# An attention and expert kernel: the attention steps of batches 2 to 7 in another order and spacing, and one finishing step split over two items

## The chip, the cores and the metric

The kernel runs on one core of a Trainium2 chip. The core has TensorE (PE, matrix products), VectorE (DVE), ScalarE (ACT), GpSimd (POOL) and SyncE (SP, which issues most of the transfers). The metric is device time of the whole kernel in microseconds, as the median of several runs; less is better.

## The reference

Two stages. An attention without a score matrix (softmax of q over its 64 features, softmax of k over its 576 positions) gives x, and a gated feed-forward layer follows:

```python
q_s = softmax(q, over head_dim);  k_s = softmax(k, over seq)      # q, k, v: 8 x 8 x 576 x 64
kv  = einsum('bhsd,bhse->bhde', k_s, v)
x   = einsum('bhsd,bhde->bhse', q_s, kv)  ->  4608 x 512
h   = x @ w_in                                                    # 512 x 2048
sp  = max(h, 0) + log1p(exp(-abs(h)))
out = (h * erf(sp)) @ w_out                                       # 2048 x 512
```

## The kernel before

**The layer's work is cut into 48 items.** The 4608 rows of x come as 12 blocks of 384 (three to a pair of batches), and each block takes four items, one for each group of 512 hidden features. Item n multiplies block n//4 by its group of w_in (`mm1`, called with k = 0 to 3), takes softplus and erf (`softplus`, `erf`, through `act`), multiplies and halves into two f16 parts (`gmul`, `ghi`, `glo`), and multiplies by w_out (`mm2`, called for three row tiles). Values are held as two f16 halves, so each product takes three passes. `mm1` needs only seven products of half size instead of eight; they go to three accumulation banks: `pY_n`, `pX_n` and `pZ_n`, of which `pX` is used for four of the seven. Each product must be read out before its bank's next one may start: VectorE reads at L1015 (Y), L1017 and L1025 (X, first and third), L1028 (Z, second), ScalarE at L1020 (Z, first), L1022 and L1030 (X, second and fourth). The line numbers are those of the kernel before.

**x is made by the attention of each batch**, a generator `attention(b)` that is run one step at a time between the products of the items. For one batch it takes k's maximum over the positions (`k_max`, elementwise on VectorE into `asc`), transposes it on TensorE (`kT_b`, L528), reduces it on VectorE (`km_b`, L532), spreads it again over the rows on TensorE (`kB_b`, L543), subtracts it from k's two halves and its tail (`k_b_0` and `k_b_1` at L709, `kt` at L714), subtracts q's maximum from q's two halves (`q_b_0` and `q_b_1`: maximum at L464, subtraction at L465; odd batches also have `qt`, the tail), takes the exponentials (L348 through `act`), multiplies k by v (`kv_b_0`, `kv_b_1`, L564), normalizes q and turns it (`turn` or `rw`, L629 and L630), and makes x (L685, copied into the block `x_i` at L453).

**What sets the order.** Each step ends with a `yield` of its share, a number from `SHARES`, and `pace` runs steps until the sum of the shares reaches a goal that grows evenly with the items. The Tile scheduler then puts the instructions of each engine in a row, so that neighbours in the code may change places. All exponentials and the softplus and erf of items 2 to 36 are held in one chain, in the order in which they are written. Once a block is whole, `finish` (two calls, k = 0 and 1) cuts it into the operands `x7_i` of `mm1`: k = 0 makes parts 0 to 2, k = 1 does four subtractions (L392) and makes parts 3 to 6, each part as a first half on ScalarE (L299) and a second on VectorE (L300). Products Y and the first X read parts 0 and 1, the first Z reads part 3. From item 9 on both calls stand in the item with n % 4 == 2; `x7_2`, for items 8 to 11, is called for in item 7 by the hand-written table `SPLITS`.

Of the kernel before, what the change touches and what calls it, by code (L numbers as in the profile page):

```python
# [13 lines left out]
ALU = mybir.AluOpType  # L14
# [41 lines left out]
def attn_moe_kernel(  # L56
# [21 lines left out]
    NG = NF // FG  # L78
# [3 lines left out]
    NBK = PT // T  # L82
# [260 lines left out]
    def act(out_, in_, func, chain=True, **kw):  # L343

        with ExitStack() as es:
            if chain and last[0] is not None:
                es.enter_context(tc.issue_after(last[0]))
            i = nc.scalar.activation(out_, in_, func, **kw)  # L348
        if chain:
            last[0] = i.ins  # L350
        return i
# [19 lines left out]
    x_next = [1]  # L371
# [77 lines left out]
    def bank(name):  # L449
        return psa.tile([P, 512], F32, tag="bk", name=name)  # L450
# [4 lines left out]
    def hd(t):  # L455
        return t.rearrange("p h d -> p (h d)")

    def rows(t):
        return t.rearrange("p t h d -> p (t h) d")

    def q_sub(t, g, name):

        m = at.tile([P, g], F32, tag=f"qm{g}", bufs=1, name=f"{name}_m")
        nc.vector.tensor_reduce(m, t, axis=AX.X, op=ALU.max)  # L464
        nc.vector.tensor_tensor(  # L465
            t, t, m[:, :, None].to_broadcast([P, g, D]), op=ALU.subtract
        )
# [44 lines left out]
    def k_max(b, ks, kt):  # L512

        kmax = asc[:, 0].rearrange("p (h d) -> p h d", h=H)
        k2 = asc[:, 1].rearrange("p (t h d) -> p t h d", t=2, h=4)
        for hf in range(2):
            nc.vector.tensor_tensor(k2, ks[hf][:, 0:2], ks[hf][:, 2:4], op=ALU.max)
            nc.vector.tensor_tensor(
                kmax[:, hf * 4:hf * 4 + 4, :], k2[:, 0], k2[:, 1], op=ALU.max
            )  # L520
        nc.vector.tensor_tensor(kmax[kt[1]], kmax[kt[1]], kt[0], op=ALU.max)
        return kmax

    def k_max_T(b, kmax):
        bk = bank(f"kT_{b}")
        km2 = hd(kmax)
        for c in range(NC4):
            nc.tensor.transpose(  # L528
                bk[:, c * P:(c + 1) * P], km2[:, c * P:(c + 1) * P], ident
            )  # L530
        km = at.tile([P, NC4], F32, tag="km", bufs=1, name=f"km_{b}")
        nc.vector.tensor_reduce(  # L532
            km, bk.rearrange("p (c s) -> p c s", c=NC4), axis=AX.X, op=ALU.max
        )
        return km
# [14 lines left out]
    def kv_mm(b, hf):  # L550


        d, kt_ = bat[b], bat[b - b % 2]["kt"]
        bk = bank(f"kv_{b}_{hf}")
        for c in range(2):
            for t in range(TM + 1):
                for a in range(2):
                    h = 2 * a + c
                    if t < TM:
                        kk, vv = d["k"][hf][:, t, h, :], d["v"][hf][:, h, t, :]  # L560
                    else:

                        kk, vv = kt_[:, 4 * hf + h, :], vtail[:, 4 * hf + h, :]
                    nc.tensor.matmul(  # L564
                        bk[a * D:(a + 1) * D, c * W:(c + 1) * W], kk, vv,
                        start=(t == 0), stop=(t == TM),
                    )
        return bk
# [7 lines left out]
    def kv_norm(b, hf, bk):  # L576
        if b < E32:
            kvf = kv32[b]
        else:
            kvf = asc[:, 0, :NC4 * D].rearrange("p (c e) -> p c e", c=NC4)  # L580
        bat[b]["kvf"] = kvf
        bkv = bk[:, :2 * W].rearrange("p (c w) -> p c w", c=2)
        rd = at.tile([P, 2, 1], F32, tag="rd", bufs=1, name=f"rd_{b}_{hf}")
        nc.vector.tensor_scalar_add(rd, bkv[:, :, D:], 1e-9)
        nc.vector.reciprocal(rd, rd)
        cs = slice(2 * hf, 2 * hf + 2)
        nc.vector.tensor_tensor(
            kvf[:, cs, :], bkv[:, :, :D], rd.to_broadcast([P, 2, D]), op=ALU.mult
        )
# [107 lines left out]
    def attention(b):  # L697
        d, j, p = bat[b], b % 2, b // 2
        even = bat[b - j]
        tl = slice(j * TAIL, (j + 1) * TAIL)  # L700
        ks, qs, kt = d["k"], d["q"], even["kt"][tl]
        kmax = k_max(b, ks, (kt, tl))
        yield SHARES[0]
        km = k_max_T(b, kmax)
        q_sub(rows(qs[0]), 16, f"q_{b}_0")
        yield SHARES[1]
        kb = k_max_rows(b, km)
        for hf in range(2):
            nc.vector.tensor_tensor(  # L709
                ks[hf], ks[hf],  # L710
                kb[:, None, hf * 4:hf * 4 + 4, :].to_broadcast([P, TM, 4, D]),
                op=ALU.subtract,
            )
        nc.vector.tensor_tensor(kt, kt, kb[tl], op=ALU.subtract)  # L714
        yield SHARES[2]
        q_sub(rows(qs[1]), 16, f"q_{b}_1")
        if j == 1:
            q_sub(even["qt"], H, f"qt_{p}")
        yield SHARES[3]
        for t in (*ks, kt, qs[0], qs[1], *([even["qt"]] if j == 1 else [])):  # L720
            act(t, t, AF.Exp, chain=b > 1)
        yield SHARES[4]
        kv_norm(b, 0, kv_mm(b, 0))
        if b > 1:
            d["v"].append(load_half(v, "v", b, 1))
        q_norm(rows(qs[0]), 16, f"q_{b}_0", b)
        yield SHARES[5]
        if b >= QDMA:
# [74 lines left out]
    def attention_rest():  # L803
        for b in range(1, B):
            yield from attention(b)
# [407 lines left out]
    def pace(at_n):  # L1213


        at_n += LEAD
        k = NBK * NG + NG
# [11 lines left out]
    FIN = 2  # L1229
    for n in range(N32, N + 2):  # L1230
        m0, m1, m2 = n < N, n - 1 < N, n - 2 < N
        if m1:
            tok(f"U{n - 1}")
        for i in range(4):
            if m0:
                tok(f"m{n}.{i}")
            if N32 < n <= N and i < 2:
                tok(f"{'IO'[i]}{n - 1}")
            if m0 and n % NG == FIN and n > 2 * NG and i < 2 and x_next[0] < NP * NBK:
                tok(f"f{fi[0]}")  # L1240
                fi[0] += 1
            if m2 and i < 3:
                tok(f"M{n - 2}.{i}")
                pace(n + (i + 1) / NTT)
        for o in SPLITS.get(n, "").split():
            tok(o)
        if m0:
            tok(f"T{n}")
            tok(f"G{n}")
# [32 lines left out]
```

## Time and profile before

| | us |
|---|---|
| median of 3 runs | 829.68 |
| the runs | 829.53 to 832.42 |
| the profiled execution, its own time | 833.75 |
| span in the profile of that execution | 831.9 |
| TensorE busy | 805.1 (97% of the span) |
| VectorE busy | 626.3 (75%) |
| ScalarE busy | 503.1 (60%) |
| mean granted TensorE clock | 0.997 |

The profile shows one execution. Engines run side by side and wait for each other through semaphores; an idle time is put down to the instruction that ended it. The profiled execution is 4.07 us above the median of the runs. Times within the profile count from the start of the span.

### The profile page before, as it was taken

Reading aid. Unit: us, or ns where it says so; the run is one execution under the profiler, and the core shown is the slowest. Engines: PE = TensorE matmul, PEld = TensorE weight load, DVE = VectorE, ACT = ScalarE, POOL = GpSimd, SP = SyncE. Lnnn points to the kernel's source line nnn. Section 1 sums busy time; section 2 is a strip of 40 time slices with the busy share of each in tenths; the row PEclk is TensorE's granted clock in tenths of the full one; section 3 lists DMA queues with packets and bytes.
Section 4 is the critical chain, followed back from the end, with each engine's and each line's share of the span. In section 5 each row is a group of like instructions: output and inputs, shape, how many; then the busy total and the mean of one; then the engine's idle time right before and its main releaser. Section 6 shows DMA issues by size and latency. Waiting matters only on the chain.

```text
span 831.9 us, 15626 instructions
## 1 busy us (share of the span) xinstructions
PE 805.1 (97%) x6594; PEld 546.3 (66%) x6594; DVE 626.3 (75%) x892; ACT 503.1 (60%) x642; POOL 15.9 (2%) x37
## 2 busy tenths in 40 slices
PE   5999999999899999999999999999999999999996
PEld 4555456666676667667667667766776767767762
DVE  6999799999987869757976679857875656544643
ACT  3697678885676566546744646655764555544432
POOL 2101000000000000000000000000000000000000
PEclk9999999999999999999999999999999999999999
DMA  9996721053136206111371205311230100100101
GB/s 260 408 224 181 189 48 39 2 132 72 45 85 129 74 7 142 50 26 28 91 128 43 65 1 106 92 26 27 64 52 14 39 1 2 39 1 2 39 1 39
DMA packets 145509, 62.61 MB, mean 75 GB/s; under 512 B 134688, under 2 KB 136736, under 8 KB 145440
## 3 DMA queue, kind: packets, MB, share of 16 engines
q1 hardware_dynamic: 143264, 53.23, 26.3%
q0 software_dynamic: 2176, 8.39, 2.9%
q8 instruction: 52, 0.85, 0.4%
q14 instruction: 17, 0.14, 0.0%
HBM read 45.09 MB, written 9.44 MB: 66 GB/s over the span
## 4 chain that ended last, share of the span: by engine, by line
PE 55%; DVE 26%; ACT 8%; issue 4%; DMA 4%; SPq 2%; POOL 0%; ACTq 0%; DVEq 0%; POOLq 0%
PE o L1129 26%; PE pX L1003 13%; PE pZ L1003 7%; DVE G L1083 3%; PE pY L1003 3%; DVE H L1101 3%; ACT G L348 3%; ACT L348 2%; DVE wt L300 2%; SPq L419 2%; DVE x L300 2%; DVE H L1097 2%; PE pX L1042 1%; DVE wt L326 1%; DVE q L478 1%
## 5 line engine op out<-in xcount | busy, mean ns | idle before, releaser
L1129 PE MATMUL o<-wt,H 128*128 128x512 f16 x1548 | 355.8, 379 | 1.8 <-DVE H L1097 1.3
L1003 PEld LDWEIGHTS <-wt 128*128 128x128 f16 x3612 | 301.5, 98 | 38.9 <-issue 16.3
L1129 PEld LDWEIGHTS <-H 128*128 128x128 f16 x1548 | 149.2, 98 | 154.0 <-DVE H L1097 1.8
L1003 PE MATMUL pX<-x,wt 128*128 128x192 f16 x2064 | 199.5, 246 | 5.3 <-DVE H L1025 2.6
L348 ACT ACT_TABLE_LOAD x104 | 133.4, 1283 | 9.3 <-DVE H L1028 7.5
L1083 DVE SCALAR_TENSOR_TENSOR G<-G,small,H 128x1536 f32<-128x1536 f32 x44 | 79.9, 1816 | 53.1 <-ACT G L348 52.8
L1030 ACT COPY H<-pX 128x384 f32<-128x384 f32 x43 | 20.4, 474 | 140.5 <-PE pX L1003 132.4
L1003 PE MATMUL pZ<-x,wt 128*128 128x192 f16 x1032 | 101.2, 248 | 0.0
L348 ACT ACTIVATE G<-H,U 128x768 f32<-128x768 f32 (+1 forms) x58 | 71.0, 1242 | 22.1 <-DVE H L1028 21.5
L1101 DVE TENSOR_TENSOR H<-G,H 128x1536 f16<-128x1536 f32 x43 | 75.5, 1755 | 0.9
L348 ACT ACTIVATE G<-G 128x1536 f32<-128x1536 f32 x48 | 71.2, 1484 | 0.5
L1003 PE MATMUL pY<-x,wt 128*128 128x192 f16 x516 | 49.6, 246 | 0.1
L453 ACT ACTIVATE x<-x 128x384 f32<-128x384 f32 (+1 forms) x52 | 16.2, 397 | 48.4 <-PE x L685 48.4
L1028 DVE TENSOR_TENSOR H<-pZ,H 128x384 f32<-128x384 f32 x43 | 23.7, 551 | 26.2 <-PE pZ L1003 26.2
L1015 DVE COPY H<-pY 128x384 f32<-128x384 f32 x43 | 23.8, 552 | 25.7 <-PE pY L1003 25.7
L1097 DVE CAST H<-G 128x1536 f16<-128x1536 f32 x43 | 41.1, 956 | 0.8
L299 ACT ACTIVATE x<-x 128x768 f16<-128x768 f32 (+1 forms) x44 | 32.9, 764 | 13.6 <-DVE x L392 13.5
L300 DVE SCALAR_TENSOR_TENSOR x<-x,x 128x768 f16<-128x768 f32 (+1 forms) x44 | 37.3, 851 | 3.2 <-ACT x L299 3.2
L1145 DVE TENSOR_SCALAR ob<-o,V 128x512 f32<-128x512 f32 x29 | 21.7, 747 | 19.7 <-PE o L1129 19.7
L1017 DVE TENSOR_TENSOR H<-pX,H 128x384 f32<-128x384 f32 x43 | 23.8, 554 | 12.9 <-PE pX L1003 12.1
L464 DVE TENSOR_REDUCE q_m<-q 128x16 f32<-128x1024 f32 x14 | 17.1, 1219 | 15.7 <-DMA q<-in_q_dram 15.6
L1042 PE MATMUL pX<-x,wt 128*128 128x384 f32 x80 | 28.3, 488 | 0.2 <-DVE wt L219 0.2
(183 smaller groups left out, 784.7 us busy)
## 6 DMA issues: line engine op xcount, KB each, us to landing
out_dram<-ob SPq DMA_DIRECT2D x32, 256.0 KB, 2.3
vbuf<-in_v_dram SPq DMA_DIRECT2D x56, 128.0 KB, 3.2
q<-in_q_dram SPq DMA_DIRECT2D x56, 128.0 KB, 3.2
k<-in_k_dram SPq DMA_DIRECT2D x56, 128.0 KB, 3.5
wt<-in_moe_w_out_dram POOLq DMA_DIRECT2D x5, 1024.0 KB, 7.4
wt<-in_moe_w_in_dram SPq DMA_DIRECT2D x4, 1024.0 KB, 12.3
wt<-in_moe_w_out_dram SPq DMA_DIRECT2D x2, 1024.0 KB, 15.9
H_raw<-in_k_dram SPq DMA_DIRECT2D x2, 512.0 KB, 5.0
```

Source lines behind the costliest of these rows:

```text
L299: nc.scalar.activation(hi, src, AF.Copy, scale=s)
L300: nc.vector.scalar_tensor_tensor(lo, src, s, hi, op0=ALU.mult, op1=ALU.subtract)
L348: i = nc.scalar.activation(out_, in_, func, **kw)
L1003: nc.tensor.matmul(o, w[wl][:, c, a * P:(a + 1) * P], x[:, xl, xi, c, :], start=(new and a == 0 and c == 0 and i == 0), stop=(c == 1 and i ...
L1015: nc.vector.tensor_copy(C[0, 0], bank2("Y"))
L1017: add(C[0, 0], bank2("X"), C[0, 0], op=ALU.add)
L1028: add(C[0, 1], bank2("Z"), C[0, 1], op=ALU.add)
L1042: nc.tensor.matmul(ph[:, :T], w[:, c, a * P:(a + 1) * P], x[:, c, :], start=(c == 0), stop=(c == NC4 - 1),)
L1083: nc.vector.scalar_tensor_tensor(flat(s["G"]), flat(s["G"]), GA32 if n < N32 else GA[:, g:g + 1], flat(s["H"]), op0=ALU.mult, op1=ALU.mult,)
L1097: nc.vector.tensor_copy(flat(s["gh"]), flat(s["G"]))
L1101: nc.vector.tensor_tensor(flat(s["gl"]), flat(s["G"]), flat(s["gh"]), op=ALU.subtract)
L1129: nc.tensor.matmul(o, s[gt][:, a, ts_], w[wl][:, a, :], start=(first_ and a == 0 and i == 0), stop=(last_ and a == FG - 1 and i == 2),)
```

## The change

For batches 2 to 7 `attention` gets five shares of its own, `EVEN`, in place of the first four of `SHARES` (sums 2.76 in both). Before, a step of 2.51 stood behind `k_max`, then kT, km and the first half of q, kB and k's subtractions right behind, and 0.16 later the second half of q. Now kT and km come 0.8 behind `k_max`, kB and k's subtractions 0.8 later, the first half of q 0.5 later, the second half with the tail 0.4 later, and 0.26 later the exponentials. The exponentials and all later steps stand as before. Batches 0 and 1 keep the old order. `finish` is now called with k = 0 in the item with n % 4 == 2 and with k = 1 in the one with n % 4 == 3 (from item 9 on), each behind the second product call (i == 1). No instruction is added or removed.

```diff
+EVEN = [0.8, 0.8, 0.5, 0.4, 0.26]
...
-        yield SHARES[0]
-        km = k_max_T(b, kmax)
-        q_sub(rows(qs[0]), 16, f"q_{b}_0")
-        yield SHARES[1]
-        kb = k_max_rows(b, km)
-        for hf in range(2):
-            nc.vector.tensor_tensor(
...
-        nc.vector.tensor_tensor(kt, kt, kb[tl], op=ALU.subtract)
-        yield SHARES[2]
-        q_sub(rows(qs[1]), 16, f"q_{b}_1")
-        if j == 1:
-            q_sub(even["qt"], H, f"qt_{p}")
-        yield SHARES[3]
...
+        else:
+
+            yield EVEN[0]
+            km = k_max_T(b, kmax)
+            yield EVEN[1]
+            k_sub(k_max_rows(b, km))
+            yield EVEN[2]
+            q_subs(0)
+            yield EVEN[3]
+            q_subs(1)
+            yield EVEN[4]
...
-            if m0 and n % NG == FIN and n > 2 * NG and i < 2 and x_next[0] < NP * NBK:
+            if m0 and n % NG >= FIN and n > 2 * NG and i == 1 and x_next[0] < NP * NBK:
```

The scheduler makes of it the following rows at three places. The numbers at the end of a tile's name tell its buffers apart. In the rows of after, lines up to L700 stand one higher than before, and those of `mm1`, `gmul`, `ghi`, `glo` 18 higher (L1043 is L1025 of before, L1101 is L1083, L1115 is L1097, L1119 is L1101); k's subtractions are L706 and L711.

First, VectorE in items 19 and 20, batch 5. Before:

```order
L1083 SCALAR_TENSOR_TENSOR G_19_3727<-G_19_3727,small_81,H_19_3566 128x1536
L300 SCALAR_TENSOR_TENSOR x7_6_4115<-x_6_3503,x7_6_4115 128x768
L1097 CAST H_19_3566<-G_19_3727 128x1536
L1025 TENSOR_TENSOR H_20_3732<-pX_20_3747,H_20_3732 128x2x192
L1101 TENSOR_TENSOR H_19_3566<-G_19_3727,H_19_3566 128x1536
L300 SCALAR_TENSOR_TENSOR x7_6_4115<-x_6_3503,x7_6_4115 128x768
L532 TENSOR_REDUCE km_5_3844<-kT_5_3839 128x4
L1028 TENSOR_TENSOR H_20_3732<-pZ_20_3774,H_20_3732 128x2x192
```

After:

```order
L1101 SCALAR_TENSOR_TENSOR G_19_3727<-G_19_3727,small_81,H_19_3558 128x1536
L393 TENSOR_TENSOR x_6_3495<-x_6_3495 128x2x192
L1115 CAST H_19_3558<-G_19_3727 128x1536
L706 TENSOR_TENSOR k_5_0_3165<-k_5_0_3165,kB_5_3821 128x1024
L1119 TENSOR_TENSOR H_19_3558<-G_19_3727,H_19_3558 128x1536
L706 TENSOR_TENSOR k_5_1_3170<-k_5_1_3170,kB_5_3821 128x1024
L711 TENSOR_TENSOR kt_2_2214<-kt_2_2214,kB_5_3821 64x512
L1043 TENSOR_TENSOR H_20_3732<-pX_20_3747,H_20_3732 128x2x192
L1046 TENSOR_TENSOR H_20_3732<-pZ_20_3781,H_20_3732 128x2x192
```

The maxima `km_5` and the three subtractions from k (L706, L711) now stand ahead of the third readout of X of item 20 (L1043), and the conversions of `x7_6` (L301) behind it.

Second, ScalarE in item 15, batch 4. Before:

```order
L1020 COPY H_15_2833<-pZ_15_2885 128x2x192
L1022 COPY H_15_2833<-pX_15_2848 128x2x192
L348 ACT_TABLE_LOAD
L348 ACTIVATE k_4_0_2204<-k_4_0_2204 128x1024
L348 ACTIVATE k_4_1_2209<-k_4_1_2209 128x1024
L348 ACTIVATE kt_2_2214<-kt_2_2214 64x512
L348 ACTIVATE q_4_0_2411<-q_4_0_2411 128x1024
L348 ACTIVATE q_4_1_2636<-q_4_1_2636 128x1024
L1030 COPY H_15_2833<-pX_15_2848 128x2x192
```

After:

```order
L349 ACT_TABLE_LOAD
L349 ACTIVATE k_4_0_2204<-k_4_0_2204 128x1024
L349 ACTIVATE k_4_1_2209<-k_4_1_2209 128x1024
L349 ACTIVATE kt_2_2214<-kt_2_2214 64x512
L349 ACTIVATE q_4_0_2411<-q_4_0_2411 128x1024
L349 ACTIVATE q_4_1_2636<-q_4_1_2636 128x1024
L1038 COPY H_15_2843<-pZ_15_2893 128x2x192
L1040 COPY H_15_2843<-pX_15_2858 128x2x192
L630 CAST rw_86<-q_4_0_2411 128x1024
L1048 COPY H_15_2843<-pX_15_2858 128x2x192
```

The five exponentials and their table load moved ahead of the first two readouts of item 15 (L1038 and L1040).

Third, VectorE at the end of batch 2's steps, where block 2 is finished for item 8. Before:

```order
L585 RECIPROCAL rd_2_1_1399<-rd_2_1_1399 128x2
L1028 TENSOR_TENSOR H_7_1217<-pZ_7_1309,H_7_1217 128x2x192
L587 TENSOR_TENSOR asc_85<-kv_2_1_1378,rd_2_1_1399 128x128
L300 SCALAR_TENSOR_TENSOR x7_2_1450<-x_2_787,x7_2_1450 128x768
L630 TENSOR_TENSOR turn_0_1374<-q_2_0_775,turn_0_1374 128x1024
L593 TENSOR_REDUCE mx_2_1420<-asc_85 128x1
L1015 COPY H_8_1470<-pY_8_1471 128x2x192
L471 TENSOR_REDUCE q_2_1_r_1567<-q_2_1_803 128x16
```

After:

```order
L588 TENSOR_TENSOR asc_85<-kv_2_1_1378,rd_2_1_1399 128x128
L393 TENSOR_TENSOR x_2_787<-x_2_787 128x2x192
L594 TENSOR_REDUCE mx_2_1420<-asc_85 128x1
L393 TENSOR_TENSOR x_2_787<-x_2_787 128x2x192
L1033 COPY H_8_1470<-pY_8_1471 128x2x192
L393 TENSOR_TENSOR x_2_787<-x_2_787 128x2x192
L472 TENSOR_REDUCE q_2_1_r_1567<-q_2_1_803 128x16
L393 TENSOR_TENSOR x_2_787<-x_2_787 128x2x192
L301 SCALAR_TENSOR_TENSOR x7_2_1450<-x_2_787,x7_2_1450 128x768
L1035 TENSOR_TENSOR H_8_1470<-pX_8_1485,H_8_1470 128x2x192
L301 SCALAR_TENSOR_TENSOR x7_2_1450<-x_2_787,x7_2_1450 128x768
```

The subtractions on `x_2` (L393), and with them the last two conversions of `x7_2` (L301), stood ahead of these rows before and now stand among L594 (the maximum of kv), the readouts of item 8 and the sum over `q_2_1` (L472).

## Rows read from the trace of the kernel before

**Rows 1.** Page of the profile, part 1: busy us of each engine (share of the span) and its instructions.
```profile
PE 805.1 (97%) x6594; PEld 546.3 (66%) x6594; DVE 626.3 (75%) x892; ACT 503.1 (60%) x642; POOL 15.9 (2%) x37
```

**Rows 2.** The view of who waited for whom, TensorE alone, from 130 to 830 us. Columns: the engine and line that waited, what released it, us in total, times, the longest in us.
```profile
PE pX L1003 <- DVE H L1025: 2.6, 4, 1.2
PE kB L543 <- DVE km L532: 2.0, 1, 2.0
PE pX L1003 <- ACT H L1022: 1.7, 2, 1.4
...
PE kv L564 <- ACT k L348: 0.6, 1, 0.6
```

**Rows 3.** The timeline of TensorE, one row at batch 3's spreading of the maxima (`kB_3`). Columns: start us, us, engine, line, operation, tiles, shape, count, and in brackets the idle time in us just before it with what released it.
```profile
225.50 0.70 PE L543 MATMUL kB<-ident,km 128*128 128x128 f32 x4 [2.04 <-DVE km L532]
```

**Rows 4.** Busy time by stretch, around the two longest gaps of TensorE. Columns: stretch and its us, then busy us and count of PE, PEld, DVE, ACT, POOL, the granted TensorE clock (1.00 is 2.4 GHz), DMA share, GB/s.
```profile
226.00:227.00 1.00, 1.00 (x9) 0.95 (x7) 0.77 (x1) 0.00 (x0) 0.00 (x0) 0.50 0.00 0
227.00:228.00 1.00, 1.00 (x8) 0.95 (x7) 1.00 (x2) 0.51 (x1) 0.00 (x0) 0.50 0.00 0
228.00:230.00 2.00, 2.00 (x18) 1.92 (x17) 1.84 (x3) 1.90 (x3) 0.00 (x0) 0.65 0.00 0
400.00:402.00 2.00, 0.65 (x8) 0.65 (x8) 2.00 (x3) 2.00 (x3) 0.00 (x0) 1.00 0.00 0
```

**Rows 5.** The same view for the 20 us in which batch 2's last steps lie.
```profile
180.00:200.00 20.00, 19.64 (x163) 13.19 (x161) 20.00 (x37) 13.52 (x14) 0.00 (x0) 1.00 0.45 93
```

**Rows 6.** The timeline of VectorE from the last step of `x7_2` (177.70 us) on. Columns as in rows 3; the tile names are without their numbers (`x<-x,x` is `x7_2`).
```profile
177.70 0.95 DVE L300 SCALAR_TENSOR_TENSOR x<-x,x 128x768 f16<-128x768 f32 x1
178.57 1.22 DVE L630 TENSOR_TENSOR turn<-q,turn 128x1024 f16<-128x1024 f32 x1
179.70 0.41 DVE L593 TENSOR_REDUCE mx<-asc 128x1 f32<-128x256 f32 x1
180.03 0.54 DVE L1015 COPY H<-pY 128x384 f32<-128x384 f32 x1
180.50 1.20 DVE L471 TENSOR_REDUCE q_r<-q 128x16 f32<-128x1024 f32 x1
```

**Rows 7.** The timeline of TensorE: the first product of item 8 that reads the second half of `x7_2` (`pZ_8`).
```profile
182.33 1.15 PE L1003 MATMUL pZ<-x,wt 128*128 128x192 f16 x12
```

**Rows 8.** Page, part 5: the group of the half conversions on ScalarE. Columns: line, engine, operation, tiles and shape, count, then busy us and mean ns of one, then the idle time just before them and what ended most of it.
```profile
L299 ACT ACTIVATE x<-x 128x768 f16<-128x768 f32 (+1 forms) x44 | 32.9, 764 | 13.6 <-DVE x L392 13.5
```

**Rows 9.** Groups of instructions by line, VectorE: the subtraction for k's tail. Columns as in rows 8.
```profile
L714 DVE TENSOR_TENSOR kt<-kt,kB 64x512 f32<-64x512 f32 x7 | 4.8, 683 | 0.1
```

**Rows 10.** The timeline of VectorE in items 19 and 20, with batch 5's steps (`q_5_1`, `km_5`, `k_5_0`). Columns as in rows 3.
```profile
379.97 1.22 DVE L464 TENSOR_REDUCE q_m<-q 128x16 f32<-128x1024 f32 x1 [1.80 <-DMA q<-in_q_dram]
...
381.58 1.22 DVE L465 TENSOR_TENSOR q<-q,q_m 128x1024 f32<-128x1024 f32 x1
...
383.18 1.74 DVE L392 TENSOR_TENSOR x<-x 128x384 f32<-128x384 f32 x3
384.84 1.81 DVE L1083 SCALAR_TENSOR_TENSOR G<-G,small,H 128x1536 f32<-128x1536 f32 x1
...
387.44 0.95 DVE L1097 CAST H<-G 128x1536 f16<-128x1536 f32 x1
388.30 0.55 DVE L1025 TENSOR_TENSOR H<-pX,H 128x384 f32<-128x384 f32 x1
388.77 1.75 DVE L1101 TENSOR_TENSOR H<-G,H 128x1536 f16<-128x1536 f32 x1
...
391.31 0.68 DVE L532 TENSOR_REDUCE km<-kT 128x4 f32<-128x512 f32 x1
...
395.66 1.21 DVE L709 TENSOR_TENSOR k<-k,kB 128x1024 f32<-128x1024 f32 x1
```

**Rows 11.** The timeline of TensorE in the same place: the last X product of item 20, a Y product, a part of mm2, `kB_5`, a Z product, and the third X product of item 21 with the 1.39 us ahead of it.
```profile
389.23 1.15 PE L1003 MATMUL pX<-x,wt 128*128 128x192 f16 x12
390.22 1.15 PE L1003 MATMUL pY<-x,wt 128*128 128x192 f16 x12
...
392.20 2.75 PE L1129 MATMUL o<-wt,H 128*128 128x512 f16 x12
394.79 0.60 PE L543 MATMUL kB<-ident,km 128*128 128x128 f32 x4
395.23 1.15 PE L1003 MATMUL pZ<-x,wt 128*128 128x192 f16 x12
...
401.35 0.82 PE L1003 MATMUL pX<-x,wt 128*128 128x192 f16 x8 [1.39 <-ACT H L1022]
```

**Rows 12.** The timeline of ScalarE in item 15, with batch 4's exponentials. Columns as in rows 3; the rows `k<-k` and `q<-q` hold two instructions each.
```profile
302.60 0.48 ACT L1022 COPY H<-pX 128x384 f32<-128x384 f32 x1 [0.46 <-PE pX L1003]
303.10 1.28 ACT L348 ACT_TABLE_LOAD   x1
307.58 2.19 ACT L348 ACTIVATE k<-k 128x1024 f32<-128x1024 f32 x2 [3.20 <-DVE k L709]
...
310.20 1.99 ACT L348 ACTIVATE q<-q 128x1024 f32<-128x1024 f32 x2
```

**Rows 13.** The timeline of TensorE at the last X product of item 14, in batch 4.
```profile
294.43 0.74 PE L1003 MATMUL pX<-x,wt 128*128 128x192 f16 x7 [1.22 <-DVE H L1025]
```

**Rows 14.** The timeline of VectorE: `q_7_1`'s maxima, with the wait for its load ahead of it. Columns as in rows 3.
```profile
570.40 1.22 DVE L464 TENSOR_REDUCE q_m<-q 128x16 f32<-128x1024 f32 x1 [0.34 <-DMA q<-in_q_dram]
```

More of the change, by code (lines that the diff above doesn't have):

```diff
@@ L702, in attention, with k_sub, q_subs @@
         kmax = k_max(b, ks, (kt, tl))
-        yield SHARES[0]
-        km = k_max_T(b, kmax)
-        q_sub(rows(qs[0]), 16, f"q_{b}_0")
-        yield SHARES[1]
-        kb = k_max_rows(b, km)
-        for hf in range(2):
-            nc.vector.tensor_tensor(
[L710 to L713, printed above, removed]
-        nc.vector.tensor_tensor(kt, kt, kb[tl], op=ALU.subtract)
-        yield SHARES[2]
-        q_sub(rows(qs[1]), 16, f"q_{b}_1")
-        if j == 1:
-            q_sub(even["qt"], H, f"qt_{p}")
-        yield SHARES[3]
+        def k_sub(kb):
+            for hf in range(2):
+                nc.vector.tensor_tensor(
+                    ks[hf], ks[hf],
+                    kb[:, None, hf * 4:hf * 4 + 4, :].to_broadcast([P, TM, 4, D]),
+                    op=ALU.subtract,
+                )
+            nc.vector.tensor_tensor(kt, kt, kb[tl], op=ALU.subtract)
+        def q_subs(i):
+            q_sub(rows(qs[i]), 16, f"q_{b}_{i}")
+            if i == 1 and j == 1:
+                q_sub(even["qt"], H, f"qt_{p}")
+        if b < 2:
+            yield SHARES[0]
+            km = k_max_T(b, kmax)
+            q_subs(0)
+            yield SHARES[1]
+            k_sub(k_max_rows(b, km))
+            yield SHARES[2]
+            q_subs(1)
+            yield SHARES[3]
+        else:
+            yield EVEN[0]
+            km = k_max_T(b, kmax)
+            yield EVEN[1]
+            k_sub(k_max_rows(b, km))
+            yield EVEN[2]
+            q_subs(0)
+            yield EVEN[3]
+            q_subs(1)
+            yield EVEN[4]
         for t in (*ks, kt, qs[0], qs[1], *([even["qt"]] if j == 1 else [])):
```

## The prediction

> **What bounds the kernel now.** I read the page first, then who TensorE waited for, then the timelines at those places. TensorE is busy 97% of the span [rows 1], and from 130 to 830 us it waits little: 2.6 us for the third X readout, 2.0 us once for `km_3`, 1.7 us for the second X readout on ScalarE, 0.6 us for k's exponentials [rows 2]. One of these costs more than its length: behind the 2.04 us gap ahead of `kB_3` [rows 3] the granted clock falls to 0.50 (1.2 GHz) for two microseconds and is 0.65 in the two after them [rows 4], so 2 x 0.50 + 2 x 0.35 = 1.7 us more are lost. The gap of 1.39 us at 400 us left the clock at 1.00 [rows 4, 11]. No instruction comes or goes, so the change can only remove such gaps or make others. All that it can take away is 2.6 + 2.0 + 1.7 + 0.6 + 1.7 = 8.6 us. What a new gap costs depends on how long a step that now stands ahead of a readout keeps its bank: one X bank serves four products of an item.
>
> Around batch 2 VectorE is full: 20.00 of 20 us from 180 us on [rows 5]. There whatever moves forward pushes something back by its whole length.
>
> **The change part by part.** All sums are of how much later TensorE does the same products, against the times of before.
>
> *Batch 2.* k's steps move forward, and block 2's finishing falls behind them. In the new order the last conversion of `x7_2` stands behind the turn (1.22), the maximum of kv (0.41), item 8's two first readouts (0.54 each) and the sum over `q_2_1` (1.20), which all stood behind it [rows 6]. That is 3.9 us by durations, some 3.5 by starts, which lie 0.08 closer. The conversion ended at 178.65, so it now ends near 182.1 if nothing else waits. But the two ScalarE conversions ahead of it, 0.76 each [rows 8], can only begin behind the last subtraction, and half of a softplus stands between them: 1.5 to 3.5 more, so 183.6 to 185.6. Item 8's first Z product, at 182.33 [rows 7], reads those parts: +1.3 to +3.3, and zero if the old stall for k's exponentials (0.6) and some slack cover it. I take **+2.5**, near the upper end, since both engines are full there.
>
> *Batch 3.* `km_3` moves ahead of two conversions (0.95 each, as in [rows 6]), L1097 and L1101 (0.95 and 1.75 as in [rows 10]), so it is done 0.95 + 0.95 + 0.95 + 1.75 less four overlaps of 0.08, about 4.3 us earlier. `kB_3`, however, moves ahead of an X product and one of mm2's three parts, 0.99 + 2.6 = 3.6 us by starts [rows 11]. Its gap shrinks from 2.04 to 2.04 - 4.3 + 3.6 = 1.3, and the clock's 1.7 go with it. Then L1025 of item 10 stands behind three subtractions from k, 1.21 + 1.21 + 0.68 [rows 9, 10], and the fourth X product waits some 1.4 for it. Sum 1.3 + 1.4 - 2.04 - 1.7 = -1.0; with the old 0.3 ahead of L1022 gone, **-1.3**. Bounds: -3.7 (only the old gap goes) and +0.4 (the clock falls all the same).
>
> *Batch 4.* The gap of 1.22 before the last X product of item 14 [rows 13] becomes shorter, as kT and kB fill part of it. But L1028 of item 14 now stands behind the three subtractions, 2.9 us later, and with it softplus, erf and the exponentials. Those come ahead of L1020 and L1022 of item 15: four exponentials of 2.19 + 1.99 and the tail's [rows 12]. So the third X product of item 15 waits about 0.3 for L1022 and the fourth 0.7 for L1025, behind q's sums (1.20 each, as in [rows 6]); the old gap of 1.22 shrinks to 0.8 in return. 0.3 + 0.7 - 0.4 = **+0.6**; bounds -1.2 (the old gap goes and nothing comes) and +2.9 (the whole delay of L1028 arrives at TensorE).
>
> *Batch 5.* Here the order decides. Behind `q_5_1`'s subtraction, which began at 381.58 [rows 10], VectorE now has `km_5` (0.68), a conversion and two subtractions (0.58 each), L1083 (1.81), a subtraction (0.58), L1097 (0.95), `k_5_0` (1.21), L1101 (1.75), `k_5_1` (1.21), the tail (0.68, [rows 9]) and only then L1025 (0.55): with 0.08 off each, 10.3 us from 382.7, done near 393.3. It was done at 388.85. The last X product of item 20 stood at 389.23 [rows 11]; kB (0.44 by starts) and eight of twelve Y products (8/12 of 0.99) now come ahead of it, so it is due at 390.3 and waits **3.1**. The old 1.39 in front of item 21's third X product [rows 11] is absorbed by this, as the exponentials are early enough: net **+1.7**. Lower bound 0.2 (kT, kB and Y fill more), upper 3.1 (the exponentials delay L1022 as before). Because this gap exceeds 2.04, I add one fall of the clock: **+1.7** [rows 4].
>
> *Batch 6* has batch 4's order again: **+0.6**. *Batch 7* has batch 5's, but its maxima waited 0.34 for their load instead of 1.80 [rows 10, 14], so VectorE is 1.5 us earlier: its gap is 3.1 - 1.5 = 1.6, no old gap is given back, and the clock stays: **+1.6**.
>
> *q last.* In batches 3 to 7 the scheduler still puts `q_b_1`'s maximum and subtraction ahead of `km_b`; only the code has q last. So the wait for `q_5_1`'s load, 1.80 us [rows 10], still holds up everything that was moved forward. *The finishing in two items*: from block 3 on, the four subtractions and two conversions move back by less than an item (831.9 / 48 = 17 us), while the first product that reads them stands in the item after. I cost it at **0**; if that cover were gone, at one gap of about 1 us a block. SP's and POOL's rows stay nearly as they were, so no load moves.
>
> *Sum:* 2.5 - 1.3 + 0.6 + 1.7 + 1.7 + 0.6 + 1.6 = **+7.4**. Against the profiled execution 833.75 + 7.4 = 841.2; on the scale of the median, 4.07 lower, **837.1**.
>
> One rule of the Trainium skill bears on the clock: Perfetto Trace Analysis, Matmul Optimizations, says that the engine scales its power with its use, so that products must run back to back. Taken as it stands it would count a fall behind each of the five new gaps above 1 us, 5 x 1.7 instead of 1 x 1.7, so +14.2 and 843.9 on the median; the gap of 1.39 us without a fall [rows 4] speaks against that.
>
> **The rivals.** *The old gaps just go* (faster). Mechanism: kT, km and kB earlier mean that TensorE never waits for `km`, and k's exponentials are ready before kv. It pays if L1025 is done within about 1 us of its product's turn in every batch, that is, if the semaphores let the scheduler's rows run denser than I walked them. Price: up to 8.6 us, so 833.75 - 8.6 - 4.07 = 821.1; with half, 825.4. For it: rows 2 name just the waits that the change moves. Against it: the row of VectorE in item 20.
>
> By the Trainium skill (Perfetto Trace Analysis, Optimization Strategy) one finds the gaps of the most used engine and lets what they wait for start sooner, which the change does; by that it is this rival that comes, 821 to 825.
>
> *Even* (no change). New gaps of 1 to 1.5 us replace those of before one for one: batch 2's finishing fits into slack, the clock falls nowhere. Then 7.4 - 2.5 - 1.7 = +3.2 or less, 829.7 to 832.9.
>
> *More falls* (slower still). Batch 2's gap of up to 3.3 is also longer than 2.04, and batch 7's nearly is: two more falls and batch 2's upper end, 7.4 + 3.4 + 0.8 = +11.6, so 841.3; with batch 5 at its upper bound 842.7.
>
> **How the numbers follow.** Forecast (new gaps with one fall, 833.9 to 840): 0.44. More falls (840 to 845): 0.14. Even (825.5 to 833.8): 0.26. Faster (below 825.5): 0.16. The likeliest gives 837.1. The range 825 to 844 leaves out most of the faster case and the tail of the slowest, under 2 in 10; the forecast's own range is 833.9 to 840. Half a per cent, 4.1 us, is about what a measurement of this kernel can tell from no change: faster 0.16, same 0.26, slower 0.58.
>
> **What would show it.** Right: TensorE waits 2.5 to 3.4 us for L1025 of item 20, with a granted clock of 0.50 behind it; 1.3 to 1.9 us at the same place of item 32; 1 to 3 us before `pZ_8`; the waits for `km` fall to 1.5 us or less; L1025 stays the largest releaser, with 6 us or more in place of 2.6. Wrong: if L1025's total stays near 2.6, the even or the faster case holds; if the gap at `kB_3` stays above 2, the clock's loss stays as well; if item 20's gap is there and the clock isn't touched, 1.7 us of the sum fall.

## The result and the profile after

The changed kernel takes 840.51 us (median of 4 runs, 839.11 to 841.24), the kernel before 831.03 us beside it: ratio 1.009 with a 95% interval of 1.0062 to 1.0118. It is slower by 5 to 10 us (the ratio stands for 7.5, the two medians are 9.5 apart); 7.4 had been forecast. The spans of the two profiled executions, 831.9 and 837.3 us, are only 5.4 us apart: the profiled execution of before took 833.75 us, longer than its timed runs, that of after 839.11, its shortest. So what these two profiles show adds up to 5.4 us, not to the whole of the loss.

Busy times hardly moved; TensorE's answer to [rows 1]:

```profile
PE 805.8 (96%) x6594; PEld 546.1 (65%) x6594; DVE 627.9 (75%) x892; ACT 502.4 (60%) x642; POOL 15.9 (2%) x37
```

So the time is in waits. The view of who waited for whom, TensorE from 130 us on, answers to [rows 2] (L1043 is L1025 of before, L1040 is L1022, L533 is L532; L1038 is L1020 and L300 is L299):

```profile
PE pX L1021 <- DVE H L1043: 6.9, 7, 2.8
PE pX L1021 <- ACT H L1040: 2.0, 2, 1.3
...
PE kB L544 <- DVE km L533: 1.3, 1, 1.3
...
PE pZ L1021 <- ACT H L1038: 0.5, 1, 0.5
PE pZ L1021 <- ACT x L300: 0.5, 1, 0.5
```

The third X readout now holds TensorE for 6.9 us where it was 2.6; the wait for `km` fell from 2.0 to 1.3, the one for k's exponentials is gone, and readouts on ScalarE (L1040 and L1038) hold it for 2.5 us where L1022 held it for 1.7.

Batch 5, the timeline of TensorE, answers to [rows 11]: `kB_5`, then the fourth X product of item 20 with its gap, then the first X product of item 21.

```profile
384.17 0.60 PE L544 MATMUL kB<-ident,km 128*128 128x128 f32 x4
...
389.18 0.82 PE L1021 MATMUL pY<-x,wt 128*128 128x192 f16 x8
392.82 1.26 PE L1021 MATMUL pX<-x,wt 128*128 128x192 f16 x12 [2.82 <-DVE H L1043]
393.88 0.84 PE L1021 MATMUL pY<-x,wt 128*128 128x192 f16 x4
394.51 0.63 PE L1147 MATMUL o<-wt,H 128*128 128x512 f16 x1
394.94 2.12 PE L1021 MATMUL pX<-x,wt 128*128 128x192 f16 x12
```

and VectorE there, which answers to [rows 10]:

```profile
379.53 1.22 DVE L465 TENSOR_REDUCE q_m<-q 128x16 f32<-128x1024 f32 x1 [1.85 <-DMA q<-in_q_dram]
...
381.13 1.22 DVE L466 TENSOR_TENSOR q<-q,q_m 128x1024 f32<-128x1024 f32 x1
382.26 0.69 DVE L533 TENSOR_REDUCE km<-kT 128x4 f32<-128x512 f32 x1
...
384.39 1.81 DVE L1101 SCALAR_TENSOR_TENSOR G<-G,small,H 128x1536 f32<-128x1536 f32 x1
...
386.59 0.96 DVE L1115 CAST H<-G 128x1536 f16<-128x1536 f32 x1
387.46 1.22 DVE L706 TENSOR_TENSOR k<-k,kB 128x1024 f32<-128x1024 f32 x1
388.59 1.75 DVE L1119 TENSOR_TENSOR H<-G,H 128x1536 f16<-128x1536 f32 x1
390.26 1.22 DVE L706 TENSOR_TENSOR k<-k,kB 128x1024 f32<-128x1024 f32 x1
391.49 0.69 DVE L711 TENSOR_TENSOR kt<-kt,kB 64x512 f32<-64x512 f32 x1
392.21 0.56 DVE L1043 TENSOR_TENSOR H<-pX,H 128x384 f32<-128x384 f32 x1
```

`km_5` and the three subtractions from k (387.46, 390.26, 391.49) stand ahead of L1043, which begins at 392.21; ahead of all of them VectorE waited 1.85 us for the load of `q_5_1`. TensorE was done with the Y products at 390.00 and starts the X product at 392.82. The busy time by stretch (columns as in [rows 4]) shows the granted clock behind that gap at 0.50:

```profile
392.00:393.00 1.00, 0.18 (x3) 0.18 (x3) 0.97 (x3) 0.00 (x0) 0.00 (x0) 1.00 0.00 0
393.00:394.00 1.00, 1.00 (x13) 0.99 (x11) 1.00 (x2) 0.00 (x0) 0.00 (x0) 0.86 0.00 0
394.00:396.00 2.00, 2.00 (x13) 1.59 (x12) 1.44 (x3) 1.85 (x3) 0.00 (x0) 0.50 0.03 8
396.00:398.00 2.00, 2.00 (x12) 1.32 (x11) 0.56 (x1) 1.98 (x2) 0.00 (x0) 0.72 0.00 0
```

Batch 7 has the same gap, 1.38 us, behind a load that was waited for 0.41 us (rows of TensorE, then of VectorE; [rows 14]):

```profile
586.48 1.15 PE L1021 MATMUL pX<-x,wt 128*128 128x192 f16 x12 [1.38 <-DVE H L1043]
```

```profile
573.18 1.22 DVE L465 TENSOR_REDUCE q_m<-q 128x16 f32<-128x1024 f32 x1 [0.41 <-DMA q<-in_q_dram]
```

Batch 3: `kB_3` waits 1.31 ([rows 3] had 2.04), and the fourth X product of item 10 now waits 1.35.

```profile
220.98 0.65 PE L544 MATMUL kB<-ident,km 128*128 128x128 f32 x4 [1.31 <-DVE km L533]
...
227.56 1.15 PE L1021 MATMUL pX<-x,wt 128*128 128x192 f16 x12 [1.35 <-DVE H L1043]
```

Batch 4, TensorE: the gap of [rows 13] is 0.49, and the third X product of item 15 waits 1.33 for L1040. ScalarE behind it ([rows 12]) shows why: L1038 and L1040 come directly behind the exponentials.

```profile
293.36 1.15 PE L1021 MATMUL pX<-x,wt 128*128 128x192 f16 x12 [0.49 <-DVE H L1043]
...
308.88 0.82 PE L1021 MATMUL pX<-x,wt 128*128 128x192 f16 x8 [1.33 <-ACT H L1040]
```

```profile
303.68 2.00 ACT L349 ACTIVATE k<-k 128x1024 f32<-128x1024 f32 x2
...
306.11 1.99 ACT L349 ACTIVATE q<-q 128x1024 f32<-128x1024 f32 x2
308.00 0.46 ACT L1038 COPY H<-pZ 128x384 f32<-128x384 f32 x1
308.36 0.47 ACT L1040 COPY H<-pX 128x384 f32<-128x384 f32 x1
```

Batch 2: the last conversion of `x7_2` on VectorE began at 182.68 (177.70 in [rows 6]), and `pZ_8` at 182.36 (182.33 in [rows 7]).

```profile
181.34 0.95 DVE L301 SCALAR_TENSOR_TENSOR x<-x,x 128x768 f16<-128x768 f32 x1
...
182.68 0.95 DVE L301 SCALAR_TENSOR_TENSOR x<-x,x 128x768 f16<-128x768 f32 x1
```

```profile
182.36 0.24 PE L1021 MATMUL pZ<-x,wt 128*128 128x192 f16 x1 [0.50 <-ACT x L300]
...
183.69 1.07 PE L1021 MATMUL pZ<-x,wt 128*128 128x192 f16 x11
```

One product of `pZ_8` ran at 182.36, behind ScalarE's half of the part; the other eleven came at 183.69, behind VectorE's last conversion (done at 183.63), and TensorE filled the time between with a product of mm2 and eight of X.

To place the loss I take, in each trace, the start of the x products of every batch half on TensorE and the time between two such marks. A batch's column runs from the last x products of the batch ahead of it to its own first ones (batch 2's from batch 1's first to its own last ones); the stretches between the two halves of a batch, 16 to 20 us, are left out, as they differ by less than 0.25 us. Worked out from the traces, in us:

```
kernel            batch 2  batch 3  batch 4  batch 5  batch 6  batch 7   behind it
before             103.80    53.31    76.59    76.24    76.13    74.80      172.54
after              103.81    51.85    77.46    79.55    76.02    77.45      172.54
```

53.31 and 79.55 each hold one fall of the clock. Batch 5 lost 3.3 us and batch 7 2.7, batch 4 0.9; batch 3 gained 1.5.

### The profile page after: what moved, and what is told of

Its sections match the earlier page's. It is cut to its first block, busy times and chain, and to the rows that moved or that the text cites. A ratio compares the mean times of both kernels' runs of the same rounds, so it can differ in the third digit from the quotient of the medians.

```text
span 837.3 us, 15629 instructions
## 1 busy us (share of the span) xinstructions
PE 805.8 (96%) x6594; PEld 546.1 (65%) x6594; DVE 627.9 (75%) x892; ACT 502.4 (60%) x642; POOL 15.9 (2%) x37
## 4 chain that ended last, share of the span: by engine, by line
PE 52%; DVE 25%; ACT 10%; issue 5%; DMA 4%; SPq 3%; ACTq 0%; POOL 0%; DVEq 0%; POOLq 0%
PE o L1147 25%; PE pX L1021 14%; PE pZ L1021 6%; ACT L349 3%; PE pY L1021 3%; ACT G L349 3%; DVE G L1101 3%; DMA q<-in_q_dram 2%; SPq L420 2%; DVE H L1119 2%; DVE x L301 2%; DVE k L706 1%; DVE H L1115 1%; DVE q L479 1%; DVE wt L301 1%
## 5 line engine op out<-in xcount | busy, mean ns | idle before, releaser
L1101 DVE SCALAR_TENSOR_TENSOR G<-G,small,H 128x1536 f32<-128x1536 f32 x44 | 79.9, 1817 | 63.5 <-ACT G L349 63.4
L1048 ACT COPY H<-pX 128x384 f32<-128x384 f32 x43 | 20.4, 474 | 161.2 <-PE pX L1021 156.5
L1119 DVE TENSOR_TENSOR H<-G,H 128x1536 f16<-128x1536 f32 x43 | 75.5, 1757 | 0.9
L1046 DVE TENSOR_TENSOR H<-pZ,H 128x384 f32<-128x384 f32 x43 | 23.7, 551 | 26.2 <-PE pZ L1021 26.2
L1115 DVE CAST H<-G 128x1536 f16<-128x1536 f32 x43 | 41.2, 957 | 0.8
L301 DVE SCALAR_TENSOR_TENSOR x<-x,x 128x768 f16<-128x768 f32 (+1 forms) x44 | 37.1, 852 | 3.6 <-ACT x L300 3.5
L300 ACT ACTIVATE x<-x 128x768 f16<-128x768 f32 (+1 forms) x44 | 33.1, 764 | 4.4 <-DVE x L393 4.2
```

The costliest lines, as they stand in the source:

```text
L300: nc.scalar.activation(hi, src, AF.Copy, scale=s)
L301: nc.vector.scalar_tensor_tensor(lo, src, s, hi, op0=ALU.mult, op1=ALU.subtract)
L1046: add(C[0, 1], bank2("Z"), C[0, 1], op=ALU.add)
L1101: nc.vector.scalar_tensor_tensor(flat(s["G"]), flat(s["G"]), GA32 if n < N32 else GA[:, g:g + 1], flat(s["H"]), op0=ALU.mult, op1=ALU.mult,)
L1115: nc.vector.tensor_copy(flat(s["gh"]), flat(s["G"]))
L1119: nc.vector.tensor_tensor(flat(s["gl"]), flat(s["G"]), flat(s["gh"]), op=ALU.subtract)
```

## The experiments

All ratios are to the kernel before run on the same chip, with 95% intervals. Each kernel's own profile is one execution.

### The finishing alone (e1)

```diff
 (kernel before)
-            if m0 and n % NG == FIN and n > 2 * NG and i < 2 and x_next[0] < NP * NBK:
+            if m0 and n % NG >= FIN and n > 2 * NG and i == 1 and x_next[0] < NP * NBK:
```

> The kernel before with finish alone in two items, the attention steps in their old order. Theory (k's subtractions ahead of the third X readout cost the time, the finishing costs nothing): ratio 0.998 to 1.002. Rival (the finishing in two items costs part of it): 1.004 or more, with gaps of TensorE ahead of the first Z product of a block.

Measured: 831.55 us against 832.31, ratio 0.9995 (0.9981 to 1.0009). The finishing costs nothing. The trace showed something else: `kB_3` waited the same 2.04 us as in [rows 3], and the granted clock stayed at 1.00 (timeline of TensorE, then busy time by stretch):

```profile
225.99 0.65 PE L543 MATMUL kB<-ident,km 128*128 128x128 f32 x4 [2.04 <-DVE km L532]
```

```profile
226.00:227.00 1.00, 1.00 (x11) 0.99 (x12) 0.72 (x2) 0.00 (x0) 0.00 (x0) 1.00 0.00 0
...
228.00:230.00 2.00, 2.00 (x23) 1.75 (x21) 1.94 (x3) 1.93 (x2) 0.00 (x0) 1.00 0.00 0
```

Batch 3 took 51.66 us here. What after seemed to gain in batch 3 is a clock that fell in the profiled execution of before and not in this one; without the fall, after's 51.85 is no gain.

How often the clock falls can be read from the runs, as each has its mean granted clock on record. In the thirteen profiled executions (those of before, after and the experiments e1 to e11 below) it is 0.998 or less in the four whose trace shows a fall (before, after, e2, e3) and 0.999 or more in the nine others. Of the 56 runs of the kernel before that were taken beside the experiments, 32 have 0.998 or less, and on each of the three chips their median lies 1.1 to 2.2 us above that of the others. Where `kB_3`'s wait is gone or 1.3 us (e4, e10, e11) it is 1 of 36, and in the changed kernel (after and e9) 3 of 10. By this mark a fall comes in more than half of the runs of the kernel before, and the one behind item 20's gap in the profile of after is the rarer case.

### The order of steps alone (e2)

```diff
 (changed kernel)
-            if m0 and n % NG >= FIN and n > 2 * NG and i == 1 and x_next[0] < NP * NBK:
+            if m0 and n % NG == FIN and n > 2 * NG and i < 2 and x_next[0] < NP * NBK:
```

> The five shares and the new order of steps for batches 2 to 7, with finish in one item as before. Theory: all of the loss stays, ratio 1.009 to 1.012, and the gap in item 20 is 2.5 to 3.2 us. Rival (the finishing costs part): 1.005 or less.

Measured: 839.71 us, ratio 1.0083 (1.0067 to 1.0099): the loss stays within the noise, and item 20's gap is 2.73. The ratio lies just below the stated band, its interval reaches into it; the rival is out.

### Batches 5 and 7 alone (e3), and all but these (e10)

```diff
 (order of steps alone; e3)
-        if b < 2:
+        if b not in (5, 7):
 (changed kernel; e10)
-        if b < 2:
+        if b < 2 or b in (5, 7):
```

> The new order for batches 5 and 7 alone, finish as before. Theory: these two bring batch 5's 3.3 us (2.8 of gap less the old 1.4, and a fall of the clock) and batch 7's 2.7: 5 to 7 us more, ratio 1.006 to 1.009. Rival (the loss is spread over all batches in small waits): 2 to 3 us more, ratio 1.004 or less.

> The changed kernel with the old order of steps in batches 5 and 7 and the new one in 2, 3, 4 and 6. Theory (batches 5 and 7 carry some 5.3 of the loss, 2.6 each): ratio 1.001 to 1.004. Rival (the loss lies as much in the others): 1.005 or more.

Measured: e3 1.0055 (1.0035 to 1.0075), 837.99 us; e10 1.0015 (1.0002 to 1.0027), 833.74 us. Of after's 9 thousandths, batches 5 and 7 carry some 5.5 and the others 1.5: the two add up to 7.0, within the intervals. e3's ratio is a little below the expected 1.006, e10's is as expected. In e10 the old order of batches 5 and 7 brings back the old times (76.11 and 74.87 us by marks).

### What stands ahead of L1025 (e5, e6)

```diff
 (changed kernel; e5: k's subtractions)
         def k_sub(kb):
+            if b in (5, 7):
+                return
 (changed kernel; e6: q's second half)
-            q_sub(rows(qs[i]), 16, f"q_{b}_{i}")
+            if i == 0 or b not in (5, 7):
+                q_sub(rows(qs[i]), 16, f"q_{b}_{i}")
```

> The changed kernel with k's three subtractions left out in batches 5 and 7 (a part of the computation is left out); all else stays. Theory (L1025 of items 20 and 32 comes late because these 3.1 us of VectorE stand ahead of it): the gaps of 2.8 and 1.4 us there shrink to 0.3 or less, 3.5 to 6 us less than the changed kernel, ratio to the kernel before 1.002 to 1.006. Rival (q's late load holds VectorE, the subtractions fill only time that is waited anyway): a gap of 1.5 us or more stays in item 20, ratio 1.007 or more.

> The changed kernel with the maxima and the subtraction of q's second half left out in batches 5 and 7 (a part of the computation is left out); k's subtractions stay. Theory (everything ahead of L1025 counts by its length): 2.4 us of work and up to 1.8 of waiting for the load go, so the gap of item 20 falls from 2.8 to 0.3 or less and that of item 32 from 1.4 to 0; ratio to the kernel before 1.002 to 1.006. Rival (k's subtractions wait for kB, whatever stands ahead): gaps of 1 us or more stay at both places.

Measured: e5 835.62 us, 1.0047 (1.0028 to 1.0066); e6 838.34 us, 1.0079 (1.0055 to 1.0103). Without k's subtractions the gap of item 32 is gone; that of item 20 is 1.14, more than the 0.3 expected. Two things took the freed time: a conversion of `x7_6` moved into it, and the scheduler put the X product ahead of the eight Y products, so TensorE asked for the bank 0.66 us earlier (TensorE in e5, where these lines stand two higher than in after):

```profile
390.28 1.15 PE L1023 MATMUL pX<-x,wt 128*128 128x192 f16 x12 [1.14 <-DVE H L1045]
```

The time came out in the expected band, but by marks batches 5 and 7 stay 1.0 and 1.2 us above the kernel before: beside these 1.14 us, the third X product of items 21 and 33 waits 0.92 us each for L1040 on ScalarE, a wait that after does not have there. Without q's second half the gaps are 1.25 and 1.25, and the time misses its band. The theory, that each step ahead counts with its full length, fails here: VectorE, freed of some 4 us, had to wait for erf before the product of item 19 (VectorE's timeline of e6, L1102 is L1083 of before):

```profile
383.01 1.82 DVE L1102 SCALAR_TENSOR_TENSOR G<-G,small,H 128x1536 f32<-128x1536 f32 x1 [0.58 <-ACT G L349]
...
386.48 1.22 DVE L706 TENSOR_TENSOR k<-k,kB 128x1024 f32<-128x1024 f32 x1
...
389.28 1.22 DVE L706 TENSOR_TENSOR k<-k,kB 128x1024 f32<-128x1024 f32 x1
390.51 0.69 DVE L711 TENSOR_TENSOR kt<-kt,kB 64x512 f32<-64x512 f32 x1
391.24 0.56 DVE L1044 TENSOR_TENSOR H<-pX,H 128x384 f32<-128x384 f32 x1
```

From this step on VectorE runs without a pause up to the readout, with k's subtractions in between; it waits nowhere for `kB_5`, so of e6's rival the sign came and not its mechanism. In these rows k's subtractions suffice for about 1 us of gap, even with q's second half gone. And e5's rival, that the late load matters, was in part right as well, as the next table shows.

### The load of q's second half (e9, the changed kernel again)

> The changed kernel once more, beside the two below. Theory (the gap of item 20 is about 1.0 us from the order plus the wait for q_5_1's load): gap less wait is 0.8 to 1.2 us again, ratio 1.008 to 1.011. Rival (the gap doesn't follow the load): gap less wait outside of this.

The same rows of VectorE between q's maximum and L1025 ran in five executions of four kernels, with the load of `q_5_1` or `q_7_1` waited for between 0 and 1.85 us. Item 32's gaps are from the same traces.

```
kernel   item 20: gap  wait  difference   item 32: gap  wait  difference
after            2.82  1.85        0.97           1.38  0.41        0.97
e2               2.73  1.76        0.97           1.01  0.00        1.01
e3               2.42  1.45        0.97           1.16  0.19        0.97
e7               1.01  0.00        1.01           1.34  0.38        0.96
e9               2.68  1.71        0.97           1.53  0.56        0.97
```

e9 itself: 839.67 us, ratio 1.0086 (1.0066 to 1.0106), as expected. The rows of e9 in item 20, TensorE, then VectorE, then the busy time by stretch behind the gap, where the granted clock stays at 1.00:

```profile
392.58 1.15 PE L1021 MATMUL pX<-x,wt 128*128 128x192 f16 x12 [2.68 <-DVE H L1043]
```

```profile
379.29 1.22 DVE L465 TENSOR_REDUCE q_m<-q 128x16 f32<-128x1024 f32 x1 [1.71 <-DMA q<-in_q_dram]
```

```profile
394.00:396.00 2.00, 1.98 (x18) 1.35 (x16) 1.71 (x3) 1.97 (x3) 0.00 (x0) 1.00 0.03 8
```

The new order costs 0.97 us at these places, and every microsecond by which the load is late comes on top, since no slack is left. The kernel before took the same wait of 1.80 us [rows 10] without a gap at this readout.

The traces of e1 and e9 make a second pair: both have the finishing in two items, e1 the old order of steps and e9 the new one, and in neither did the clock fall. Their spans are 830.9 and 837.6 us, 6.7 apart (e9 is 0.5 ahead where batch 2's column begins). By marks:

```
kernel            batch 2  batch 3  batch 4  batch 5  batch 6  batch 7   behind it
e1                 104.01    51.66    77.18    76.02    75.96    74.80      172.57
e9                 103.81    51.84    77.95    78.75    77.08    77.60      172.54
```

Batches 5 and 7 carry 2.7 and 2.8 us, batches 6 and 4 1.1 and 0.8, batches 2 and 3 next to nothing.

### The exponentials later (e7)

```diff
 (changed kernel)
-            yield EVEN[4]
+            yield EVEN[4] + 0.6
-        yield SHARES[4]
+        yield SHARES[4] - (0.6 if b > 1 else 0)
```

> The changed kernel with the exponentials 0.6 of a share later (the next step's share is 0.6 smaller), so that the first two readouts of item 15 on ScalarE stand ahead of them again. Theory (the waits for L1020 and L1022 come from the exponentials ahead of them): the gaps of 1.3, 0.7 and 0.5 us behind the kv products of batches 4, 6 and 7 go, 1.5 to 3 us less than the changed kernel, ratio 1.005 to 1.008; the gaps before the fourth X product of items 20 and 32 stay at 2.4 to 3.2 and 1.0 to 1.5. Rival (those waits come with L1028's delay): they stay, ratio 1.008 or more.

Measured: 836.66 us, 1.0053 (1.0033 to 1.0073), within the expected band. The waits for L1040 in batches 4 and 6 went, but 0.85 us for the fourth X readout (L1048, on ScalarE) came in their place, and batch 7's 0.55 stayed. By marks batch 4 kept 77.37 of 77.46 us and batch 7 77.42 of 77.45, so against after the ScalarE part of the theory isn't borne out; what this execution was shorter by lies in batch 5, 77.08 us, where the load happened to come in time and the clock stayed up. Against e9's trace batches 4 and 6 are 0.6 and 0.8 us shorter. All six runs, 835.04 to 837.79, lie below those of after, and the profiled one is the longest of them, so the cause of the whole 3 us stays open. The gap in item 20:

```profile
391.88 1.15 PE L1021 MATMUL pX<-x,wt 128*128 128x192 f16 x12 [1.01 <-DVE H L1043]
```

### k's subtractions later (e8)

```diff
 (changed kernel)
-EVEN = [0.8, 0.8, 0.5, 0.4, 0.26]
+EVEN = [0.8, 1.71, 0, 0.16, 0.09]
```

> The changed kernel with other shares for batches 2 to 7: 0.8, 1.71, 0, 0.16, 0.09, so kT and km early, kB and k's subtractions at the old place, q behind them. Theory: with k's subtractions behind L1025 of items 20 and 32 the two gaps go, ratio 0.996 to 1.003. Rival (the order of k before q is what costs): ratio 1.005 or more.

Measured: 839.65 us, 1.0119 (1.0063 to 1.0175). The two gaps of items 20 and 32 did go, as the theory said, and the time didn't come back: with k's subtractions ahead of q's in the code, they now stand right behind L1025 and ahead of L1028, so L1028 and with it softplus and erf come later, and six exponentials stand ahead of the readouts L1038 and L1040. Who waited for whom on TensorE in e8:

```profile
PE pX L1021 <- DVE H L1043: 5.9, 5, 1.9
PE pZ L1021 <- ACT H L1038: 3.2, 2, 1.6
...
PE pX L1021 <- ACT H L1040: 1.1, 1, 1.1
PE pX L1021 <- ACT H L1048: 0.9, 3, 0.5
```

L1038 has 3.2 us, in two waits of 1.6 in batches 5 and 7, and L1043 5.9, nearly all in batches 2, 3, 4 and 6. That item 20 has no gap must be read with care: the load of `q_5_1` was in time here, and e11 below, with the same rows of VectorE up to this readout, has a gap with a late load. One of the four runs, 846.48 us at a mean clock of 0.993, widens the interval; the medians are 7.5 us apart. So the time is the rival's, and the rows name what costs in this execution: k's part among the readouts, ahead of L1043 or of L1046 on VectorE and, through the exponentials, ahead of L1038 on ScalarE.

### kT and km early, all else in its old place (e4, e11)

```diff
 (kernel before)
-        yield SHARES[0]
-        km = k_max_T(b, kmax)
+        if b < 2:
+            yield SHARES[0]
+            km = k_max_T(b, kmax)
+        else:
+            yield 0.8
+            km = k_max_T(b, kmax)
+            yield SHARES[0] - 0.8
         q_sub(rows(qs[0]), 16, f"q_{b}_0")
 (e11: the same with b < 3)
```

> The kernel before with only the transposes and the reduction of k's maxima (kT, km) 0.8 behind the maxima in batches 2 to 7; the spreading, k's and q's subtractions stay where they were. Theory (it is k's three subtractions ahead of L1025 that cost, kT and km early are a gain): the 2.0 us ahead of kB_3 go with the 1.7 of the clock, no gap of over 1 us before the fourth X product of items 20 and 32: 3 to 6 us less than before, ratio 0.993 to 0.997. Rival (the early kT and km themselves push L1025 back): 3 us more or worse, ratio 1.003 or more.

> kT and km early in batches 3 to 7 alone, batch 2 as in the kernel before. Theory (batch 2 lost 1.1 us by the early kT and km, batch 3 gained): ratio 0.994 to 0.997, faster than the run with batch 2. Rival (batch 2's loss was chance): 0.998 or more.

Measured: e4 830.86 us, 0.9978 (0.9958 to 0.9998); e11 831.83 us, 0.9982 (0.9967 to 0.9996). Both beat the kernel before, by about 2 thousandths, less than expected, and batch 2 makes no difference that can be told: e11 lies in the band of its rival. The wait for `km` is gone in both. In e4's profiled execution (span 826.7 us) the load of `q_5_1` was in time and item 20 had no gap above 0.3; in e11's (831.8 us) it was waited for 1.87 us, and this gap appeared (L1030 is L1025 of before):

```profile
389.62 1.15 PE L1008 MATMUL pX<-x,wt 128*128 128x192 f16 x12 [1.72 <-DVE H L1030]
```

With the early `km`, the reduction (0.68) and L1101 (1.75) also stand ahead of this readout, so the slack for a late load is gone here too. By marks batch 3 takes 49.94 us in e4 and 51.27 in e11, against 51.66 in e1, and batch 5 74.90 and 76.67 against 76.02: with the load late, the early step pays back in batch 5 what it gains in batch 3.

## Why the prediction was right

Forecast 837.1 us against 829.68, so +7.4; measured a ratio of 1.009, which is +7.5 on 831.03, with an interval of +5 to +10 (e9, the same kernel again: 1.0086, +7.1). The direction, the size and the seat of the loss were right; several terms were not, and some of the agreement is luck. The measured 840.51 itself lies just above the forecast's own 833.9 to 840, in the band given to "more falls", whose mechanism did not come: one fall in after's trace, none in e9's. The kernel before also took 831.03 us beside it, 1.35 more than the 829.68 that the forecast stands on. By its own steps ("measured" is after against before in the profiles, then e9 against e1, where no clock fell):

- **Batch 5** was the core. Gap forecast 3.1, measured 2.82 and 2.68; net +3.4 forecast, +3.3 and +2.7 by marks. (The sum slips by 0.3: 10.3 us from 382.7 end at 393.0, and the gap is 2.7.) Shown by e3 and e10 as the seat of the loss together with batch 7. The cause has two parts, 0.97 from the order and the rest from the load, which the text named in "q last". The fall of the clock behind the gap, +1.7, came in the profiled execution, but by the mean clock only in 3 of 10 runs: as a sure term it was too large.
- **Batch 7:** gap forecast 1.6, measured 1.38 and 1.53. Net forecast +1.6, measured +2.7 and +2.8: the readout L1038 of item 33 behind the exponentials added 0.55, and the rest lies in small waits below 0.1 and in the later start of products behind each gap (1.38 us of idle time put off the next product by 1.54).
- **Batch 3:** `kB_3`'s gap 1.3 and measured 1.31, the fourth X product 1.4 and 1.35, net -1.3 and -1.5. Without a fall in either trace it is +0.2: the whole credit is the clock's 1.7. By the mean clock that fall comes in 32 of 56 runs of before, so on average about 1.0 of it counts (an estimate from these counts), and the credit was too large by about 0.5.
- **Batch 4:** net +0.6 forecast, +0.9 and +0.8 measured, with other parts: L1040 1.33 instead of 0.3, the old gap 0.49 instead of 0.8, and nothing for the fourth product.
- **Batch 6:** +0.6 forecast, -0.1 and +1.1 measured. The term rested on batch 4's order alone; the old gap of 0.76 went in after's trace, and the wait for L1040 was 0.69 there and 1.33 in e9.
- **Batch 2:** +2.5 forecast, 0.0 and -0.2 measured. This is the failed term. The last conversion ended at 183.63, the early end of the 183.6 to 185.6 that was worked out, and I took the upper part. More than that, a late conversion was counted as a wait of TensorE in full: eleven of the products of `pZ_8` did move back to 183.69, but others were put ahead of them, so the wait was 0.50 where 1 to 3 us had been named as a sign, and old gaps of the same size went.
- **The finishing:** 0 forecast, 0.9995 measured in e1.

The faster rival fell with L1043's 6.9 us, the even one with the interval of the ratio. The sum came out close because the 2.5 of batch 2 and the sure fall in batch 5, which were too much, stand against batch 3's credit and batch 7's missing 1.1; that was luck, while the place of the loss and the gaps of batches 5 and 7 were read from the rows.

What stays open is why the load of `q_5_1` comes up to 1.9 us late in nine of the twelve profiled executions that have it and in time in three (e4, e7, e8); no run here changed it.

## What to carry to other kernels

A step that moves forward on an engine that also empties accumulation banks is paid by the readouts that it passes: list them row by row, and add whatever load the moved step's engine waits for ahead of them, since spent slack turns its lateness into a gap one for one. An early step is a gain only where its result was waited for and no readout is held up by it; here the reduction alone came near to that, worth 2 thousandths, and even it used up the slack of item 20. A saving or a cost that hangs on the clock in a single profile should be weighed by the mean clock of the other runs first.

## What the hardware showed beyond that

The granted clock doesn't follow from a gap's length. After 2.04 us without a product it fell to 0.50 in one execution and not in another [rows 3, 4 and e1]; after 2.42 and 2.82 us it fell (e3, after), after 2.68 and 2.73 it didn't (e9, e2), and in e2 it fell at a gap of 3.17 us in batch 3. TensorE had run products up to each of these gaps. The Trainium skill (Perfetto Trace Analysis, Matmul Optimizations) says that the engine scales its power with its use and asks for products back to back. These traces agree so far that a fall comes at a gap, but most gaps have none. A fall costs some 1.7 us here: in after the clock is 0.86 in the microsecond from 393 us, 0.50 from 394 to 396 and 0.72 over the two after. Executions of one kernel differ by 2 us or more even where the mean clock is 1.00 (e4: 828.89 and 834.79), and the wait for a single load, 0 to 1.87 us for `q_5_1`, is one source that the traces show.
